# The last product of a fused attention and MLP kernel, moved to seven block products over stored operands

## The chip, the cores and the metric

The kernel runs on one core of one Trainium2 chip, in float32 with matmuls in the float32r form. The metric is the device time of one execution in microseconds, the median of several. Three runs of the kernel before gave 779.0, 778.12 and 778.18, a median of 778.18 us.

## The reference

Attention over 32 memory slots per head, then two MLPs. The first multiplies two projections with each other, the second has a leaky ReLU. Only the last two lines below belong to the stage that is changed; `h` and `o` are the names that the kernel uses for their two products.

```python
def _moe2_ref(x, w_in, w_out):          # x: 2304 x 512, w_in: 512 x 2048, w_out: 2048 x 512
    h = x @ w_in
    g = np.maximum(0.01 * h, h)
    return (g @ w_out).astype(np.float32)
```

The weights come as float64 and are made into float32 on the chip.

## The kernel before

Every float32 operand of a large product is split into a high part (rounded to float32r by ScalarE) and a low part (the rest, by VectorE). A product of two such operands is three matmuls: high by high, high by low, low by high (`PASSES`).

**First part of the program (to about 397 us).** Attention and the first MLP (`ab`, `x1p`) are written as steps with costs, due times and dependencies; `Plan.order` sorts them, and they are issued in that order. Steps of the same plan prepare the weights of the second MLP: `Conv` loads a float64 tile of 512 KB into one of five places called `stage`, two ScalarE operations and one VectorE operation (`join`, L273) make a float32 tile of it, and further operations split it. `plan_pair` does this for two column blocks of `w2_in`, forms the four sums S1 to S4 that Strassen's algorithm (Winograd's form) needs, splits all operands and stores them to a scratch tensor in DRAM (`a_scr`). `plan_w2o` does it for one row block of `w2_out`; 14 of the 16 blocks go through DRAM (`o_scr`), and all 16 are in SBUF from the first quads of the last stage on (`load_w2o`, L1057).

**Last stage (397 us to the end).** Tokens are taken in three rounds `r` of two blocks of 384; the 2048 inner columns in eight pairs `mp` of 128-column blocks. One (round, pair) is a quad, so there are 24. For a quad, `h` is made by seven block products in two PSUM banks (L1231, `mul`, 6 matmuls of 384 columns each), with VectorE sums between them; `leaky` (L1237) writes each of the four blocks of g as a high part and as float32, and a later VectorE subtraction (L1243) gives the low part. `emit_o` (L1247) then multiplies one block of g with its row block of `w2_out`: 9 matmuls of 512 columns (3 token groups by 3 passes, L1254), accumulated over all 16 blocks in six PSUM tiles, `o`. Four such products per quad are placed between the products of `h` of the next one. `store_out` copies a finished `o` to SBUF and writes it out.

The operands of `h` come back from DRAM for every quad: `load_ring` (L1034) refills one part of a two-deep ring as soon as the quad that used it has gone past, on SyncE's queue.

In the last stage the source order is a wish; the framework's scheduler sets the order on each engine.

Of the kernel before, what the change touches and what calls it, by code (L numbers as in the profile page):

```python
# [176 lines left out]
def kernel(  # L177
# [41 lines left out]
    TB = 384  # L219
# [3 lines left out]
    WARM = 27.0  # L223
    scale = 1.0 / float(D) ** 0.5
# [693 lines left out]
    a_scr, o_scr, a_kept, o_kept = {}, {}, {}, {}  # L918

    def plan_pair(mp, due):  # L920

        c, js = {}, []
        holds = [Hold("stage", 5), Hold("stage", 4)]
        convs = []
        for i in range(2):
            m = 2 * mp + i
            view = w2_in[:, m * 128:(m + 1) * 128].rearrange("(t p) c -> p t c", p=128)
            conv = Conv(("w2i", m), view, None, 2)
            convs.append(conv)
            load = plan.add(  # L930
                DMA, 1.46, lambda conv=conv, h=holds[i]: conv.load(f"stage{h.place}"), [s_p2], take=holds[i], due=due
            )
            v = plan.add(ACT, t_act(512), conv.high_word, [load])
            z = plan.add(ACT, t_act(512), conv.low_word, [load])
            js.append(plan.add(DVE, t_dve(512), conv.join, [v, z]))

        def a(i, k):
            return convs[i].hw.bitcast(F32).rearrange("p (a k c) -> p a k c", a=2, k=2)[:, :, k]
# [7 lines left out]
        for n, (ops, after) in enumerate((  # L946
            ((("S1", (1, 0), (1, 1), ALU.add), ("S2", "S1", (0, 0), ALU.subtract)), js),
            ((("S3", (0, 0), (1, 0), ALU.subtract), ("S4", (0, 1), "S2", ALU.subtract)), js),
        )):
            before, users = plan.slot(f"ob{n}")  # L950
            for i, (name, x, y, op) in enumerate(ops):
# [9 lines left out]
                give = [holds[z[0]] for z in {z for z in (x, y) if not isinstance(z, str)}]  # L961
                uses = [users] + [made[z].users for z in (x, y) if isinstance(z, str) and made[z].users is not users]
                made[name] = plan.add(DVE, t_dve(256), add, after + before + need, give=give, uses=uses)
                made[name].users = users
        for i, part in enumerate(PARTS):
            tag = f"X{i}"
            before, users = plan.slot(tag)
            lows = []
            for o, name in enumerate(part):

                def high(i=i, o=o, name=name, tag=tag, part=part):
                    if o == 0:
                        c["out", i] = p2[0].tile([128, len(part), 2, 2, 128], F32R, tag=tag, name="a_out")
                    act.activation(out=c["out", i][:, o, :, 0], in_=src(name), func=ACTF.Copy)

                def low(i=i, o=o, name=name):
                    t = c["out", i][:, o]
                    dve.tensor_tensor(out=t[:, :, 1], in0=src(name), in1=t[:, :, 0].bitcast(F32), op=ALU.subtract)

                direct = name[0] == "A"  # L980
# [7 lines left out]
            def store(i=i, part=part):  # L988
                t = a_scr[mp, i] = scr.tile([128, len(part), 2, 2, 128], F32, tag=f"a{mp}_{i}", name="a_scr")
                dma.dma_start(out=t, in_=c["out", i].bitcast(F32))  # L990

            a_kept[mp, i] = plan.add(DMA, 0.73 * len(part), store, lows, uses=[users], due=due)

    def plan_w2o(m, due):

        before, users = plan.slot(f"R{m % 2}")

        def make():
            t = w2o_t[m] = p2[0].tile([128, 2, DM], F32R, tag=f"R{m % 2}", name="w2o")
            return t[:, 0], t[:, 1]  # L1000

        plan_conv(Conv(("w2o", m), w2_out[m * 128:(m + 1) * 128, :], make, 2), before + [s_p2], users, due=due)
        if m >= 2:

            def store():
                t = o_scr[m] = scr.tile([128, 2, DM], F32, tag=f"o{m}", name="o_scr")
                dma.dma_start(out=t, in_=w2o_t[m].bitcast(F32))

            o_kept[m] = plan.add(DMA, 1.46, store, conv_end["w2o", m], uses=[users], due=due)

    w2o_order = [*range(2, NM), 0, 1]
    for mp in range(NP):
        due = clock[0] - 20.0 + 2.0 * mp
        plan_pair(mp, due)
        for m in w2o_order[2 * mp:2 * mp + 2]:
            plan_w2o(m, due + 6.0)
# [39 lines left out]

    def load_w2o(m):  # L1057
        if m < 4:
            if m == 2:
                w2o_t["AT"] = keep.tile([128, 2, 2, DM], F32R, tag=f"AT{B - 1}", name="w2o")  # L1060
            t = w2o_t["AT"][:, m - 2]
        else:
            tag = f"B{m - 4}" if m < 4 + FH else f"G{m - 4 - FH}"
            t = keep.tile([128, 2, DM], F32R, tag=tag, name="w2o")
        dma.dma_start(out=t.bitcast(F32), in_=o_scr[m])
        w2o_t[m] = t

    s = []
    for m in (2, 3):
        s = [plan.add(  # L1070
            DMA, 1.46, lambda m=m: load_w2o(m), ab_end[B - 1] + [o_kept[m]] + s, due=clock[0] + 8.0 * m - 10.0
        )]

# [126 lines left out]
    p2 = p2[0]  # L1200
    ps2 = ctx.enter_context(tc.tile_pool(name="ps2", bufs=1, space=bass.MemoryType.PSUM, reuse_waits="tile"))
    for m in range(4, NM):
        load_w2o(m)
    banks = [ps2.tile([128, TB], F32, tag=f"h{i}", name="h") for i in range(2)]
    w_tiles = [keep.tile([128, 2 * TB], F32, tag="W", name="sums", bufs=2) for _ in range(2)]
# [3 lines left out]
    gg_tags = [f"stage{i}" for i in range(NS) if i != s4.place]  # L1209

    sums = {"s": w_tiles[0][:, :TB], "U2": w_tiles[0][:, TB:]}
    sums["U3"] = keep.tile([128, TB], F32, tag="t0", name="U3", bufs=2)
    sums["C11"] = keep.tile([128, TB], F32, tag="t0", name="C11", bufs=2)
    u2 = [sums["U2"], keep.tile([128, TB], F32, tag="t1", name="U2")]
    O, GG = {}, {}
    o_todo, o_made = deque(), defaultdict(int)
    later = deque()

    def flush():
        while later:  # L1220
            later.popleft()()

    def mul(bank, n, i, fresh):
# [3 lines left out]
        for kp in range(2):  # L1227
            x = x_halves(op_b)
            x = x[0][:, kp] if len(x) == 1 else x[kp][:, 0]
            for hw, hx in PASSES:  # L1230
                pe.matmul(  # L1231
                    out=banks[bank], lhsT=ring[i % 2, part][:, o, kp, hw], rhs=x[:, hx],
# [4 lines left out]
    def leaky(src, g32, t, m, slot):  # L1237

        gg = GG[t, m] = keep.tile([128, 2, TB], F32R, tag=gg_tags[slot], name="gg")
        act.activation(out=gg[:, 0], in_=src, func=ACTF.Prelu, alpha=0.01)  # L1240
        act.activation(out=g32, in_=src, func=ACTF.Prelu, alpha=0.01)  # L1241
        later.append(
            lambda: dve.tensor_tensor(out=gg[:, 1], in0=g32, in1=gg[:, 0].bitcast(F32), op=ALU.subtract)  # L1243
        )
        o_todo.append((t, m))

    def emit_o(t, m, us=range(TB // 128)):  # L1247
        for u in us:
            n = o_made[t, u]
            o_made[t, u] += 1  # L1250
            if n == 0:
                O[t, u] = ps2.tile([128, DM], F32, tag=f"o{t % 2}{u}", name="o")
            for hg, hw in PASSES:
                pe.matmul(  # L1254
                    out=O[t, u], lhsT=GG[t, m][:, hg, 128 * u:128 * u + 128], rhs=w2o_t[m][:, hw],
                    start=(n == 0 and (hg, hw) == PASSES[0]), stop=(n == NM - 1 and (hg, hw) == PASSES[-1]),
                )
            if n == NM - 1:
                store_out(t * TB + u * 128, O[t, u], u)
# [3 lines left out]
    def store_out(t0, ps, u):  # L1263
        if t0 < NT - 2 * TB:
# [116 lines left out]
```

## Time and profile before

| | |
|---|---|
| median of 3 runs | 778.18 us (778.12 to 779.0) |
| profiled execution, first to last instruction | 776.8 us |
| TensorE busy | 768.3 us, 99% |
| VectorE busy | 422.1 us, 54% |
| ScalarE busy | 379.1 us, 49% |
| DRAM read, written | 103.55 MB, 26.74 MB |

The page gives the span of one profiled execution and no other time for it; the median of the timed runs is 1.4 us above that span. TensorE is busy in nearly all of the span, so the question for any change is how long its instructions take and whether it is made to wait. In the names of the trace, SPq is SyncE's DMA queue.

### The profile page before, as it was taken

How to read it: one execution, taken by the hardware profiler on the slowest of the kernel's cores; microseconds unless marked ns; L12 is line 12 of the kernel's file. 1: busy time of each engine (PE TensorE's matmuls, PEld its weight loads, DVE VectorE, ACT ScalarE, POOL GpSimd, SP SyncE). 2: the span in 40 equal slices, each digit the busy share in tenths (PEclk: the TensorE clock that was granted, in tenths of full speed). 3: DMA queues.
4: the chain of work that ended last, by engine and by line, in shares of the span. 5: the costliest groups of instructions: out<-in, count | busy, mean ns of one | idle time of the engine just before them, and what ended most of it. 6: DMA issues, size and time to landing. Idle time of an engine off the chain costs nothing.

```text
span 776.8 us, 14332 instructions
## 1 busy us (share of the span) xinstructions
PE 768.3 (99%) x5814; PEld 691.4 (89%) x5814; DVE 422.1 (54%) x813; ACT 379.1 (49%) x782; POOL 1.2 (0%) x9
## 2 busy tenths in 40 slices
PE   9999999999999999999999999999999999999997
PEld 5599899898998989898999998999999999899996
DVE  5795755646828898998742233383332364233322
ACT  4897444444948687877413223353332254223223
POOL 0000000000000000000000000000000000000000
PEclk9999999999999999999999999999999999999999
DMA  9987205103604998889357333346333336433303
GB/s 317 339 289 231 91 3 184 31 2 100 226 24 151 324 359 306 303 289 379 145 225 290 122 122 122 109 132 195 122 108 123 122 119 179 136 119 119 115 0 82
DMA packets 59265, 131.21 MB, mean 169 GB/s; under 512 B 4672, under 2 KB 27200, under 8 KB 59200
## 3 DMA queue, kind: packets, MB, share of 16 engines
q1 hardware_dynamic: 59120, 130.17, 49.7%
q8 instruction: 46, 0.75, 0.4%
q14 instruction: 19, 0.16, 0.1%
q10 hardware_dynamic: 80, 0.13, 0.0%
HBM read 103.55 MB, written 26.74 MB: 168 GB/s over the span
## 4 chain that ended last, share of the span: by engine, by line
PE 98%; ACT 1%; DVE 0%; issue 0%
PE o L1254 26%; PE h L1231 23%; PE x1p L848 20%; PE ab L791 20%; PE wp L740 3%; PE warm L1188 2%; PE km L479 1%; PE sc L623 1%; PE qT L595 1%; PE aT L690 0%; DVE AT L705 0%; PE kvT L538 0%; PE bc L432 0%; PE sc L629 0%; PE qL L573 0%
## 5 line engine op out<-in xcount | busy, mean ns | idle before, releaser
L1254 PE MATMUL o<-w2o,gg 128*128 128x512 f32 x864 | 213.6, 392 | 0.0
L1254 PEld LDWEIGHTS o<-w2o,gg 128*128 128x128 f32 x864 | 160.9, 188 | 28.8 <-DVE gg L1243 0.4
L791 PEld LDWEIGHTS ab<-AT,W 128*128 128x128 f32 x1152 | 154.0, 188 | 15.5 <-issue 4.2
L848 PE MATMUL x1p<-G,wo 128*128 128x288 f32 x1152 | 164.0, 298 | 0.0
L791 PE MATMUL ab<-AT,W 128*128 128x288 f32 x1152 | 159.7, 297 | 1.0 <-DVE W L759 0.7
L848 PEld LDWEIGHTS x1p<-G,wo 128*128 128x128 f32 x1152 | 154.7, 188 | 5.8 <-issue 3.0
L1231 PE MATMUL h<-T,ring 128*128 128x384 f32 x720 | 141.4, 337 | 0.0
L1231 PEld LDWEIGHTS h<-T,ring 128*128 128x128 f32 x720 | 127.6, 188 | 4.2 <-ACT C L1241 0.3
L1240 ACT ACTIVATE gg<-U 128x384 fp32r<-128x384 f32 x36 | 18.9, 524 | 99.6 <-DVE U L1324 80.9
L1231 PE MATMUL h<-B,ring 128*128 128x384 f32 x288 | 57.7, 336 | 0.0
L1231 PEld LDWEIGHTS h<-B,ring 128*128 128x128 f32 x288 | 51.3, 188 | 3.8
L813 DVE TENSOR_TENSOR g<-a_sb,ab 128x288 f32<-128x288 f32 x96 | 42.6, 449 | 19.2 <-PE ab L791 15.0
L1243 DVE TENSOR_TENSOR gg<-C,gg 128x384 fp32r<-128x384 f32 x24 | 13.4, 559 | 72.0 <-ACT C L1241 72.0
L1240 ACT ACTIVATE gg<-h 128x384 fp32r<-128x384 f32 x24 | 11.8, 492 | 79.4 <-PE h L1231 79.4
L261 ACT ACTIVATE stage<-stage 128x512 f32<-128x512 f32 x68 | 46.5, 684 | 7.1 <-DMA stage<-in_moe_w_out_dram 2.9
L265 ACT ACTIVATE stage<-stage 128x512 int32<-128x512 uint32 x68 | 46.3, 681 | 0.0
L808 ACT COPY a_sb<-ab 128x288 f32<-128x288 f32 x96 | 37.9, 395 | 9.1 <-PE ab L791 8.5
L759 DVE TENSOR_TENSOR W<-wp,W 128x512 fp32r<-128x512 f32 x48 | 32.4, 685 | 17.3 <-ACT W L753 16.8
L827 ACT ACTIVATE G<-g 128x576 fp32r<-128x576 f32 x48 | 33.0, 687 | 16.3 <-DVE g L813 15.9
L831 DVE TENSOR_TENSOR G<-g,G 128x576 fp32r<-128x576 f32 x48 | 36.1, 753 | 8.0 <-ACT G L827 7.7
L753 ACT ACTIVATE W<-wp 128x512 fp32r<-128x512 f32 x48 | 27.9, 598 | 20.7 <-PE wp L740 11.6
L1324 DVE TENSOR_TENSOR U<-U,h 128x384 f32<-128x384 f32 x24 | 13.3, 554 | 44.9 <-PE h L1231 44.9
(101 smaller groups left out, 656.3 us busy)
## 6 DMA issues: line engine op xcount, KB each, us to landing
ring<-a_scr SPq DMA_DIRECT2D x72, 512.0 KB, 3.5
stage<-in_moe_w_out_dram SPq DMA_DIRECT2D x28, 512.0 KB, 5.4
a_scr<-a_out SPq DMA_DIRECT2D x24, 512.0 KB, 4.6
stage<-in_moe_w_in_dram SPq DMA_DIRECT2D x16, 512.0 KB, 5.7
o_scr<-w2o SPq DMA_DIRECT2D x14, 512.0 KB, 7.9
w2o<-o_scr SPq DMA_DIRECT2D x14, 512.0 KB, 7.1
stage<-in_moe_w_a_dram SPq DMA_DIRECT2D x12, 512.0 KB, 5.8
stage<-in_moe_w_b_dram SPq DMA_DIRECT2D x12, 512.0 KB, 5.6
```

The costliest lines, as they stand in the source:

```text
L261: act.activation(out=x, in_=x, func=ACTF.Prelu, scale=2.0 ** -112, alpha=2.0 ** 32)
L265: act.activation(out=self.lw, in_=self.lw.bitcast(U32), func=ACTF.Copy, scale=7.249 / 2.0 ** 32, bias=0.25)
L759: dve.tensor_tensor(out=t[:, 1], in0=c["ps"][:, :, 256 * i:256 * i + 256], in1=t[:, 0].bitcast(F32), op=ALU.subtract)
L791: pe.matmul(out=c[x, n][:, :HS], lhsT=W[b, f][:, hw, g, 128 * x:128 * x + 128], rhs=AT[b][:, g, ha, n * HS:(n + 1) * HS], start=(g == 0 an ...
L808: act.copy(c["sb"][:, n], c[0, n][:, :HS])
L813: dve.tensor_tensor(out=c["g"][:, n], in0=c["sb"][:, n], in1=c[1, n][:, :HS], op=ALU.mult)
L827: act.activation(out=G[b, f][:, 0], in_=c["g"], func=ACTF.Copy)
L831: dve.tensor_tensor(out=t[:, 1], in0=c["g"], in1=t[:, 0].bitcast(F32), op=ALU.subtract)
L848: pe.matmul(out=c[n][:, :HS], lhsT=wo_t[f][:, hw, 128 * m:128 * m + 128], rhs=G[b, f][:, hg, n], start=(f == fs[0] and (hw, hg) == PASSES[0]),
L1231: pe.matmul(out=banks[bank], lhsT=ring[i % 2, part][:, o, kp, hw], rhs=x[:, hx], start=fresh and kp == 0 and (hw, hx) == PASSES[0], stop=k ...
L1240: act.activation(out=gg[:, 0], in_=src, func=ACTF.Prelu, alpha=0.01)
L1254: pe.matmul(out=O[t, u], lhsT=GG[t, m][:, hg, 128 * u:128 * u + 128], rhs=w2o_t[m][:, hw], start=(n == 0 and (hg, hw) == PASSES[0]), stop= ...
```

## The change

`o` is made by one level of Strassen's algorithm too (Winograd's form: seven products in place of eight).

- The blocks of g of a quad are a 2 by 2 matrix: two token blocks by two column blocks. `w2_out` of the same pair is a 2 by 2 matrix of 128 by 256 blocks. Each product is 9 matmuls of 256 columns (3 token groups by 3 passes).
- Quads are taken in chunks of four. For a chunk, product 1 is done for its four quads one after another into the same PSUM accumulator, then product 2, and so on (`o_product`, 28 steps). After each group of four, VectorE or ScalarE adds or copies 768 columns of PSUM to running totals C11, C12, C21, C22 in SBUF (`o_sums`). Two chunks make a round; then totals are stored.
- The products of `o` of a chunk are placed beside the products of `h` of the next chunk: 28 steps of one `h` product (6 matmuls) and one `o` product (9 matmuls). The first chunk has `h` alone, with its quads taken two at a time in four PSUM banks; after the last chunk `o` is alone.
- `leaky` now writes float32 alone. VectorE makes S1 to S4 of g (`g_sum`, one operation of 384 columns each), and every operand is split for itself (`g_split`: ScalarE high, VectorE low, 384 columns each).
- The operands of `w2_out` (four blocks and four sums, T1 to T4, all split) are made by `plan_pair`, stored in DRAM, and read back for each product: 168 loads of 256 KB (`load_t`), into four places at first and eight later. Four of the eight pairs are prepared in the first part of the program as before; the other four (`LATE = 4`) are prepared during the first chunks of the last stage, their steps spread between the products (0.9 of a planned microsecond per step, `tempo`).

The core of the diff:

```diff
-    def emit_o(t, m, us=range(TB // 128)):
-        for u in us:
...
-            for hg, hw in PASSES:
-                pe.matmul(
-                    out=O[t, u], lhsT=GG[t, m][:, hg, 128 * u:128 * u + 128], rhs=w2o_t[m][:, hw],
...
+    def g_split(c, k):
+        n, q = divmod(k, 4)
+        name = O_OPS[n][0]
+        src, t = g[4 * c + q, name], s_slots.popleft()
+        s_op[c, k] = t
+        act.activation(out=t[:, 0], in_=src, func=ACTF.Copy)
+        dve.tensor_tensor(out=t[:, 1], in0=src, in1=t[:, 0].bitcast(F32), op=ALU.subtract)
...
+    def load_t(c, k):
...
+        dma.dma_start(out=t.bitcast(F32), in_=o_scr[4 * (c % 2) + q, part][:, o])
...
+        for u in range(3):
+            for hs, ht in PASSES:
+                pe.matmul(
+                    out=acc[chain][:, 256 * u:256 * u + 256], lhsT=s[:, hs, 128 * u:128 * u + 128], rhs=t[:, ht],
...
+    tempo = 0.0
+    for c in range(chunks + 1):
+        for k in range(steps):
+            if c == 0:
+                pair, n = divmod(k, 14)
+                n, which = divmod(n, 2)
+                h_product(2 * pair + which, n, pairs[which], w_sets[which])
+            elif c < chunks:
+                q, n = divmod(k, 7)
+                i = 4 * c + q
+                h_product(i, n, banks, {**w_sets[0], "U2": w_sets[i % 2]["U2"]})
+                if later:
+                    later.popleft()()
+                if c % 2 and c + 1 < chunks:
+                    x_ready_next(c // 2, q, n)
+            if c:
+                o_product(c - 1, k)
+                o_ready(c - 1, k)
...
+            if now >= -AHEAD:
+                advance(now, AHEAD, g_split, s_slots)
+                advance(now, T_AHEAD, load_t, t_slots)
+            if late:
+                tempo += 0.9
+                while late and late[0].start < tempo:
+                    late.popleft().emit()
```

**TensorE, in the middle of the last stage.** Before, two products of `h` (L1231) and one of `o` (L1254) in turn:

```order
L1231 MATMUL h<-B_4874,ring 128x384 x6
L1231 MATMUL h<-T_4936,ring 128x384 x6
L1254 MATMUL o<-w2o,gg 128x512 x9
L1231 MATMUL h<-B_5000,ring 128x384 x6
L1231 MATMUL h<-T_5014,ring 128x384 x6
L1254 MATMUL o<-w2o,gg 128x512 x9
```

Now, one product of `h` (L1241) and one of `o` (L1330) in turn:

```order
L1241 MATMUL h<-B_5204,ring 128x384 x6
L1330 MATMUL o<-w2o,S 128x256 x9
L1241 MATMUL h<-T_5226,ring 128x384 x6
L1330 MATMUL o<-w2o,S 128x256 x9
L1241 MATMUL h<-B_5242,ring 128x384 x6
L1330 MATMUL o<-w2o,S 128x256 x9
```

A quad had four products of `o` and has seven; each is half as wide.

**VectorE, from the last addition of the first MLP (L869, now L871) into the first quads of the last stage.** Before, sums of `h` (L1305, L1315, L1324, L1328), low parts of g (L1243) and two sums for later rounds (L1097):

```order
L869 TENSOR_TENSOR x_2983<-x_2983,x1p 128x288 x8
L1097 TENSOR_TENSOR sums<-x_2239,x_1563 128x768
L1097 TENSOR_TENSOR T<-x_2239,sums 128x768
L1305 TENSOR_TENSOR sums<-sums,h 128x384
L1243 TENSOR_TENSOR gg<-C_5420,gg 128x384
L1315 TENSOR_TENSOR U_5419<-sums,h 128x384
L1324 TENSOR_TENSOR U_5419<-U_5419,h 128x384
```

Now the sums of `h` (L1260, L1264) stand behind work for the late pairs (sums L975, low parts L1000, join L275):

```order
L871 TENSOR_TENSOR x_2983<-x_2983,x1p 128x288
L1000 TENSOR_TENSOR w2o<-S,w2o 128x256
L1000 TENSOR_TENSOR w2o<-stage,w2o 128x256 x2
L975 TENSOR_TENSOR S<-stage 128x256
L1088 TENSOR_TENSOR sums<-x_2239,x_1563 128x768
L975 TENSOR_TENSOR S<-stage,S 128x256
L275 SCALAR_TENSOR_TENSOR stage<-stage 128x512
L975 TENSOR_TENSOR S<-stage,S 128x256
L1260 TENSOR_TENSOR sums<-sums,h 128x384
L1000 TENSOR_TENSOR w2o<-stage,w2o 128x256
L1000 TENSOR_TENSOR w2o<-S,w2o 128x256
L1260 TENSOR_TENSOR U_5419<-g,h 128x384
```

Seven instructions for the late pairs and one for a later round have come between the last addition to x and the first sum of `h` there, where two for a later round stood.

**SyncE's queue in the second chunk.** Before, ring loads alone (L1039):

```order
L1039 DMA ring<-a_scr 128x1024 x3
L1039 DMA ring<-a_scr 128x512
L1039 DMA ring<-a_scr 128x1024 x3
L1039 DMA ring<-a_scr 128x512
L1039 DMA ring<-a_scr 128x1024 x3
```

Now ring loads (L1048), stores of the late pairs (L1014) and loads of operands for `o` (L1303), in one queue:

```order
L1303 DMA w2o<-a_scr 128x512 x2
L1014 DMA a_scr<-w2o 128x512
L1048 DMA ring<-a_scr 128x1024
L1303 DMA w2o<-a_scr 128x512 x2
L1014 DMA a_scr<-w2o 128x1024
L1048 DMA ring<-a_scr 128x1024
L1303 DMA w2o<-a_scr 128x512
L1048 DMA ring<-a_scr 128x512
L1303 DMA w2o<-a_scr 128x512
L1014 DMA a_scr<-w2o 128x1024
```

A load of an operand of `o` now stands behind a store that waits for VectorE, and a ring load behind both.

## Rows read from the trace of the kernel before

**Rows 1.** Page: span, and busy time of each engine with its instructions.
```profile
span 776.8 us, 14332 instructions
...
PE 768.3 (99%) x5814; PEld 691.4 (89%) x5814; DVE 422.1 (54%) x813; ACT 379.1 (49%) x782; POOL 1.2 (0%) x9
```

**Rows 2.** Page: the chain that ended last, by engine and by line.
```profile
PE 98%; ACT 1%; DVE 0%; issue 0%
PE o L1254 26%; PE h L1231 23%; PE x1p L848 20%; PE ab L791 20%; PE wp L740 3%; PE warm L1188 2%; PE km L479 1%; PE sc L623 1%; PE qT L595 1%; PE aT L690 0%; DVE AT L705 0%; PE kvT L538 0%; PE bc L432 0%; PE sc L629 0%; PE qL L573 0%
```

**Rows 3.** Stretches: busy us (instructions) by engine, granted clock, DMA share, GB/s.
```profile
310.00:330.00 20.00, 20.00 (x165) 17.99 (x165) 18.92 (x42) 17.15 (x37) 0.00 (x0) 1.00 0.85 310
...
350.00:370.00 20.00, 20.00 (x166) 17.99 (x165) 16.73 (x34) 15.42 (x31) 0.00 (x0) 1.00 1.01 377
...
400.00:410.00 10.00, 10.00 (x52) 8.83 (x51) 4.89 (x10) 3.94 (x8) 0.00 (x0) 1.00 1.03 416
...
440.00:500.00 60.00, 60.00 (x302) 54.24 (x301) 18.98 (x35) 17.07 (x35) 0.00 (x0) 1.00 0.36 118
```

**Rows 4.** Timeline of TensorE: start us, us, then instructions merged, with count.
```profile
384.81 12.90 PE L848 MATMUL x1p<-G,wo 128*128 128x288 f32 x96
397.55 1.20 PE L1231 MATMUL h<-B,ring 128*128 128x384 f32 x6
...
440.47 1.20 PE L1231 MATMUL h<-B,ring 128*128 128x384 f32 x6
441.51 1.20 PE L1231 MATMUL h<-T,ring 128*128 128x384 f32 x6
442.56 2.21 PE L1254 MATMUL o<-w2o,gg 128*128 128x512 f32 x9
444.61 1.20 PE L1231 MATMUL h<-B,ring 128*128 128x384 f32 x6
```

**Rows 5.** 128-column transposes: their line's durations (min/median/max ns), and three in the timeline.
```profile
L595 PE MATMUL qT<-ident,q_t x64: 270/272/332, 12.1 to 177.6; 128*128 128x128 f32 x64
...
29.81 0.49 PE L595 MATMUL qT<-ident,q_t 128*128 128x128 f32 x3
```

**Rows 6.** Groups of the last stage's matmuls: count, busy us, mean ns, idle before.
```profile
L1254 PE MATMUL o<-w2o,gg 128*128 128x512 f32 x864 | 213.6, 392 | 0.0
...
L1231 PE MATMUL h<-T,ring 128*128 128x384 f32 x720 | 141.4, 337 | 0.0
...
L1231 PE MATMUL h<-B,ring 128*128 128x384 f32 x288 | 57.7, 336 | 0.0
```

**Rows 7.** DMA issues: line, count, KB each, median us to landing; last, 400 to 420 us alone.
```profile
ring<-a_scr SPq DMA_DIRECT2D x72, 512.0 KB, 3.5
...
ring<-a_scr SPq DMA_DIRECT2D x24, 256.0 KB, 2.6
...
ring<-a_scr SPq DMA_DIRECT2D x6, 512.0 KB, 9.7
```

**Rows 8.** VectorE groups by shape: busy us, mean ns of one, idle before and releaser.
```profile
L273 DVE SCALAR_TENSOR_TENSOR stage<-stage 128x512 int32<-128x512 int32 x44 | 30.2, 687 | 4.1 <-ACT stage L265 4.0
...
L1243 DVE TENSOR_TENSOR gg<-sums,gg 128x384 fp32r<-128x384 f32 x36 | 20.1, 558 | 23.9 <-ACT sums L1241 23.9
...
L1324 DVE TENSOR_TENSOR U<-U,h 128x384 f32<-128x384 f32 x24 | 13.3, 554 | 44.9 <-PE h L1231 44.9
...
L978 DVE TENSOR_TENSOR a_out<-S,a_out 128x256 fp32r<-128x256 f32 x32 | 12.8, 417 | 0.2 <-ACT a_out L974 0.2
...
L1123 DVE TENSOR_TENSOR T<-T,T 128x768 fp32r<-128x768 f32 x10 | 9.5, 950 | 0.0
```

**Rows 9.** Timeline where the first MLP ends: VectorE's last addition to x.
```profile
397.75 0.45 DVE L869 TENSOR_TENSOR x<-x,x1p 128x288 f32<-128x288 f32 x1 [1.95 <-PE x1p L848]
```

**Rows 10.** Timeline of the end: the last matmuls and the last copy.
```profile
763.85 8.61 PE L1254 MATMUL o<-w2o,gg 128*128 128x512 f32 x36
...
772.49 0.59 ACT L1269 COPY ob<-o 128x512 f32<-128x512 f32 x1 [2.13 <-PE o L1254]
```

**Rows 11.** Waits of SyncE's queue: us in total, times, longest us.
```profile
SPq L1039 <- PE h L1231: 269.6, 82, 3.8
```

More of the change, by code (lines that the diff above doesn't have):

```diff
@@ L945, in plan_pair @@
         made = {}
[L946 to L949, printed above, removed]
+        for n, ops in enumerate(sums):
             before, users = plan.slot(f"ob{n}")
@@ new lines, in o_sums @@
+    def o_sums(c, n):
+        src = acc[O_OPS[n][2]][:, :768].rearrange("p (u c) -> p u c", u=3)
+        first = c % 2 == 0
+        for name, fresh in (
+            (("C11", first),), (("C22", first),), (("C21", first),), (("C21", False),),
+            (("C22", False), ("C12", first)), () if first else (("C11", False),), (("C12", False),),
+        )[n]:
+            if fresh:
+                act.copy(total[name], src)
+            else:
+                dve.tensor_tensor(out=total[name], in0=total[name], in1=src, op=ALU.add)
+        done = {3: "C21", 4: "C22", 5: "C11", 6: "C12"}.get(n)
+        if done and not first:
+            store_out(c // 2, done)
@@ new lines, with store_out @@
+    out_v = out.rearrange("(b p j) c -> b j p c", b=B, p=64)
+    def store_out(r, name, us=range(3)):
+        row, col = int(name[1]) - 1, int(name[2]) - 1
+        for u in us:
+            for h in range(2):
+                b, j = divmod((2 * r + row) * (TB // 64) + 2 * u + h, NR)
+                queue = act if h and len(us) == 1 else dma
+                queue.dma_start(
+                    out=out_v[b, j][:, 256 * col:256 * col + 256], in_=total[name][64 * h:64 * h + 64, u]
+                )
@@ new lines, with add, late_steps @@
+    class Late(Plan):
+        def add(self, engine, cost, emit, after=(), uses=(), **kw):
+            return super().add(engine, cost, emit, [x for x in after if x is not s_p2], uses, **kw)
+    late_plan = Late(stage=0)
+    late_plan.places["stage"] = [(0.0, i) for i in places]
+    for mp in range(NP - LATE, NP):
+        late_holds = plan_pair(late_plan, "out", mp, 100.0 * mp, ("R0", "R1", f"B{FH - 2}", f"G{FH - 1}"))
+    late = deque(late_plan.order())
+    def late_steps(until):
+        while late and late[0].start < until:
+            late.popleft().emit()
@@ L1341, with advance, x_ready_next @@
+    following = {g_split: 0, load_t: 0}
+    def advance(now, ahead, make, slots):
+        while following[make] <= min(now + ahead, chunks * steps - 1) and len(slots) > 1:
+            make(*divmod(following[make], steps))
+            following[make] += 1
+    def x_ready_next(r, q, n):
+        if q == 2 and n == 6:
             for name in ("T1", "T2", "T3"):
                 t_make(r + 1, name)
-        if not last:
-            o_next()
-    flush()
-    for n in range(2):
-        rest = [x for x in o_todo if x[0] == NTB - 2 + n]
-        for u in range(TB // 128):
-            for x in rest:
-                emit_o(*x, [u])
+        if q == 3:
+            if n == 3:
+                while later:
+                    later.popleft()()
+                t_make(r + 1, "T4")
+            x_split(r + 1, X_NAMES[n], False)
+            later.append(lambda: x_split(r + 1, X_NAMES[n], True))
```

335 lines of the change are left out of this document (184 added, 151 removed).

## The prediction, made before the changed kernel ran

> **What bounds the kernel now.** First the page's busy shares: TensorE works in 99% of the span [rows 1]; then the chain of waits: 98% of it is TensorE, and the two products of the last stage are its longest entries, `o` with 26% and `h` with 23% [rows 2]. Then the stretches: at 400 to 410 and at 440 to 500 us TensorE is busy for the whole stretch at a granted clock of 1.00, the 2.4 GHz level, while VectorE has about a third of its time taken [rows 3]. The groups of the three matmul forms have no idle time before them [rows 6]. So the last stage is as long as its matmuls are, and a change there is worth what it takes out of TensorE's column time, less every wait that it brings.
>
> **Matmuls.** A matmul's own duration (392 ns for 512 columns, [rows 6]) overlaps the next one, so I take distances between starts in the timeline [rows 4]: 288 columns (397.55 - 384.81) / 96 = 132.7 ns; 384 columns (441.51 - 440.47) / 6 = 173.3 ns; 512 columns (444.61 - 442.56) / 9 = 227.8 ns. The three lie on a line of 0.42 ns per column. No matmul of 256 columns of this kind is in the trace. The line gives 132.7 - 32 x 0.423 = 119.2 ns. Its bounds are the nearest rows on both sides: not above the 132.7 of 288 columns, not below the 109 ns at which 128-column transposes follow each other ((490 - 272) / 2, [rows 5]).
>
> `o` had 864 matmuls [rows 6]: 864 x 227.8 = 196.8 us. It gets 24 quads x 7 products x 9 = 1512: 1512 x 119.2 = 180.2 us. **Gain 16.6 us**; between the bounds, from a gain of 32.0 (109 ns) to a loss of 3.8 (132.7 ns). `h` keeps its 1008 matmuls of 384 columns.
>
> **First part of the program.** VectorE loses 16 joins and 16 low parts of 512 columns, 32 x 0.687 = 22.0 us, and gets four pairs of 2 joins and 11 operations of 256 columns: 4 x (2 x 0.687 + 11 x 0.417) = 23.8 us [rows 8]. That is the same load in the same place: 0.
>
> **First chunks: two new loads at once.** The first chunk has only `h`, so a step is 6 x 173.3 = 1.04 us instead of a quad's mixture, and the four late pairs are prepared there.
>
> VectorE: between its last addition to x and the last sum of the first quad stand 15 operations of 256 columns, 2 joins, 2 of 768, 9 sums of `h` and 2 splits: 15 x 0.417 + 2 x 0.687 + 2 x 0.950 + 9 x 0.554 + 2 x 0.558 = 15.6 us [rows 8]. It starts on them 0.65 us after the first matmul of `h` (398.20 against 397.55, [rows 9, 4]), so it ends at 16.3. TensorE wants that bank for its 15th product, at 14 x 1.04 = 14.6: **1.7 us late**. The next two quads have 11 us of VectorE work for 14.6 of TensorE.
>
> DMA: from the fifth load for a late pair to the point where the operands of `o` get eight places in place of four, SyncE's queue has 4 late loads (2.1 MB), 16 late stores (7.3), 25 ring loads (11.5) and 20 operand loads (5.2): 26.2 MB. TensorE needs 48 products of `h` and 16 of `o` for that: 48 x 1.04 + 16 x 9 x 0.1192 = 67.1 us. With all engines of the DMA taken the trace shows 377 GB/s in loads mixed with stores and 416 in loads alone [rows 3]: 69.5 or 63 us, so 2.4 us too late or nothing. The lowest rate near there is 310, with a DMA share of 0.85 [rows 3]: 84.5 us, 17.4 late. I take 377, the row with the same mixture: **2.4 us**. While the queue is full a ring load lands after 9.7 us instead of 3.5 [rows 7], and with four places an operand of `o` is asked for only three products ahead, some 7 us; so the wait would be seen before products of `o`. A store that waits for VectorE holds back every load behind it in the same queue; SyncE already spends 269.6 us waiting for `h` before ring loads [rows 11]. The Trainium skill, page "DMA: Bandwidth & Descriptors", section "Where 436 GB/s comes from", says that between HBM and SBUF some 358 GB/s per core are the limit; by that figure the 26.2 MB take 73.2 us (an estimate from the page) and the wait is 6.1. The trace's 377 and 416 exceed it, so this sum does not use it.
>
> The two waits partly cover each other: together **4**, from 0 to 17.4.
>
> **Middle of the stage.** Per quad VectorE gets 7 splits, 4 sums of g and 5 sums of `h`, and totals of 768 columns: about 10 to 11 us against 7 x 1.04 + 7 x 1.073 = 14.8 on TensorE. Operand loads add 7 x 0.262 MB per 14.8 us, 124 GB/s to the 118 of now [rows 3]: 242 of 377. Both hidden: 0. ScalarE has no more than VectorE: 0.
>
> Where a round ends, the operands of the next are prepared too. In quads 8 and 9 of the 24 VectorE has 49 operations of 384 columns or their equal and 10 of 768: 49 x 0.556 + 10 x 0.950 = 36.7 us, against 14 products of `h` and 18 of `o`, 33.9: 2.8 short. In quads 16 and 17 it is 30.5 against 29.6: 0.9 short. VectorE takes its work in order, and between the last product of one quad and the first of the next there is one product of `o`, 1.07 us, for the sum that frees the bank. Together 3.7, taken as **4**; from 0 (the quads before have room) to 19.6, when all the preparation (11.1 and 8.5 us) is exposed.
>
> **End.** The last chunk has `o` alone: VectorE 25 us for TensorE's 31, and operands asked for six steps, 6.4 us, ahead of loads that land in 2.6 in this size [rows 7]. After the last matmuls came a copy and a store [rows 10], now an addition and a store. **1**.
>
> **Sum.** 776.8 - 16.6 + 4 + 4 + 1 = 769.2 for the profiled span. The median of the runs is 1.4 above the span shown, so **770.6 us**.
>
> **Rivals.**
> - *All hidden.* Both DMA and VectorE keep up, and only the matmuls change: 776.8 - 16.6 + 1 + 1.4 = 762.6. For it: the scheduler lays `o` products late in the second chunk, which gives early transfers time. Against: VectorE's counts above leave no room at two places. 20%.
> - *DMA sets the pace of the first two chunks (slower).* At 310 GB/s the wait there is 17.4: 776.8 - 16.6 + 17.4 + 4 + 1 + 1.4 = 784. It decides for slower when that wait exceeds 16.6 - 5 = 11.6 us, which is 26.2 MB at under 333 GB/s. For it: three kinds of transfers in one queue, in order, with stores that wait. Against: 377 and 416 in the trace. 17%.
> - *VectorE's order.* Half of the preparation for the next round is exposed, 9.8 in place of 4, and the first chunk stays at 4: about 776.4; with all of it 786. 10%.
> - *Weight loads do not get shorter with the columns.* Each matmul has a load of 128 columns of weights before it, and there are 648 more of them; if the pair cannot go below 132.7, `o` takes 200.6 us and the time is 776.8 + 3.8 + 9 + 1.4 = 791. Against: the 109 ns of 128-column transposes, with such a load before each. 5%. The Trainium skill, page "TensorE: Matmul & The Clock Gate", section "LDWEIGHTS (loading the stationary operand)", gives columns / 1.2 in ns, an estimate of 107 ns for 128 columns: the transposes' 109 agree with it as a floor, and 256 columns would be just above it.
>
> **Chances and range.** The forecast 48%, the rivals as given. A difference of 0.2%, 1.6 us, is about what a measurement of this kernel can tell. Faster by more than that: nearly all of the forecast (46), all hidden (20) and a little of VectorE's order (1): 67%. Within 0.2%: 7%, the edge of the forecast and part of VectorE's order. Slower: 26%, DMA, weight loads, the rest of VectorE's order and of the forecast. The range of 762 to 784 takes in the first three rivals up to their values, but neither the weight loads nor full exposure of the preparation.
>
> **What would show it.** Right: starts of 256-column matmuls about 119 ns apart; TensorE without idle time from the third chunk on except at two round ends; a DMA share of 1 for some 60 us from 397 us on, with short waits of `o` for operand loads or of `h` for VectorE. Wrong: starts at 130 ns or more; waits for DMA of over 10 us; waits spread over all quads, which would mean that banks, not preparation, hold TensorE; or a granted clock below 1.00 after a wait.

## The result, and the profile after

The changed kernel takes **772.09 us** (median of 4 runs, 770.9 to 773.19) against 778.59 for the kernel before in the same session: a ratio of 0.9913, 95% interval 0.9894 to 0.9932. It is 6.5 us faster; 7.6 were forecast. The profiled execution spans 771.4 us, 5.4 less than before; it is the slowest of the four (773.19 us), so what is read from it below accounts for 5.4 us and not for the 6.5 of the medians. The sum behind the forecast is not the sum that came out.

The page of the changed kernel: span, busy time of each engine, the chain by engine and by line, two groups of matmuls (count | busy us, mean ns of one | idle before), and the DMA issues (count, KB, median us to landing).

```profile
span 771.4 us, 16541 instructions
...
PE 753.5 (98%) x6462; PEld 709.5 (92%) x6462; DVE 549.4 (71%) x1082; ACT 424.0 (55%) x894; POOL 1.2 (0%) x9
...
PE 88%; DMA 6%; ACT 2%; DVE 2%; SPq 1%; issue 1%; ACTq 0%; DVEq 0%
PE o L1330 22%; PE ab L793 20%; PE h L1241 19%; PE x1p L850 18%; PE wp L742 3%; DMA stage<-in_moe_w_out_dram 2%; DMA w2o<-a_scr 2%; DMA stage<-in_moe_w_a_dram 1%; PE sc L625 1%; PE km L481 1%; DMA a_scr<-w2o 1%; PE qT L597 1%; PE warm L1179 1%; PE o L1311 1%; SPq L1364 1%
...
L1330 PE MATMUL o<-w2o,S 128*128 128x256 f32 x1476 | 196.8, 282 | 1.7 <-DMA w2o<-a_scr 1.7
...
L1241 PE MATMUL h<-T,ring 128*128 128x384 f32 x720 | 144.3, 337 | 2.8 <-ACT g L1251 1.6
...
w2o<-a_scr SPq DMA_DIRECT2D x168, 256.0 KB, 4.0
ring<-a_scr SPq DMA_DIRECT2D x72, 512.0 KB, 5.1
```

Where the chain was 98% TensorE [rows 2], DMA has come in with 6%, and the groups of matmuls, which had no idle time [rows 6], have some. The stretches say where it is (columns as in [rows 3]):

```profile
397.00:427.00 30.00, 27.33 (x151) 25.54 (x150) 24.18 (x53) 16.07 (x36) 0.00 (x0) 1.00 0.91 304
427.00:460.00 33.00, 30.27 (x198) 28.97 (x198) 21.63 (x48) 16.91 (x37) 0.00 (x0) 1.00 0.97 347
460.00:475.00 15.00, 14.18 (x98) 13.46 (x97) 9.47 (x20) 7.64 (x18) 0.00 (x0) 1.00 0.90 296
475.00:500.00 25.00, 24.99 (x184) 24.79 (x183) 24.01 (x44) 17.41 (x33) 0.00 (x0) 1.00 0.94 341
...
600.00:622.00 22.00, 22.00 (x159) 22.00 (x158) 21.24 (x43) 14.22 (x29) 0.00 (x0) 1.00 0.75 247
...
735.00:772.00 37.00, 29.27 (x228) 28.55 (x226) 20.14 (x35) 9.99 (x19) 0.00 (x0) 0.93 0.63 182
```

TensorE is idle for 6.2 us between 397 and 475 us, never at the two round ends, and again in the last 15 us. Between, it is full.

**Matmuls.** In the timeline of the changed kernel's TensorE, steps of `h` and `o` follow each other thus:

```profile
491.74 1.23 PE L1330 MATMUL o<-w2o,S 128*128 128x256 f32 x9
492.81 1.21 PE L1241 MATMUL h<-T,ring 128*128 128x384 f32 x6
493.86 1.22 PE L1330 MATMUL o<-w2o,S 128*128 128x256 f32 x9
```

(492.81 - 491.74) / 9 = 118.9 ns for 256 columns; over the 100 undisturbed groups of nine from 500 to 735 us the mean is 1.067 us, 118.6 ns. `h` stays at 1.05.

**The first two chunks.** ScalarE and SyncE's queue in the changed kernel's timeline, at the two longest stops of TensorE there (in brackets the idle time before the instruction and what ended it):

```profile
399.32 0.68 ACT L263 ACTIVATE stage<-stage 128x512 f32<-128x512 f32 x1 [1.28 <-DMA stage<-in_moe_w_out_dram]
399.90 0.67 ACT L267 ACTIVATE stage<-stage 128x512 int32<-128x512 uint32 x1
400.46 0.46 ACT L1258 COPY sums<-h 128x384 f32<-128x384 f32 x1
...
401.47 0.46 ACT L1258 COPY g<-h 128x384 f32<-128x384 f32 x1
...
421.03 0.43 ACT L997 ACTIVATE w2o<-stage 128x256 fp32r<-128x256 f32 x1 [4.24 <-DMA a_scr<-w2o]
421.37 0.48 ACT L1251 ACTIVATE g<-h 128x384 f32<-128x384 f32 x1
...
422.30 0.47 ACT L1251 ACTIVATE g<-h 128x384 f32<-128x384 f32 x1
```

```profile
410.92 3.57 SPq L1048 DMA_DIRECT2D ring<-a_scr  x4
414.58 0.38 SPq L1014 DMA_DIRECT2D a_scr<-w2o  x1
```

```profile
401.98 1.32 PE L1241 MATMUL h<-T,ring 128*128 128x384 f32 x6 [1.22 <-ACT g L1258]
...
422.83 7.47 PE L1241 MATMUL h<-T,ring 128*128 128x384 f32 x40 [1.41 <-ACT g L1251]
```

ScalarE takes its work in order. At 421 it splits a late operand into a place that an earlier late operand still holds, until its store has landed; that store was issued at 414.58, behind four ring loads, and took over 6 us. Behind the split stand the operations (L1251) that free `h`'s banks; TensorE goes on after the second, at 422.83. At 399 ScalarE waits for a late load, and the copies (L1258) stand behind it and behind other late work.

These are two of several stops. All waits of TensorE from 397 to 475 us (us in total, times, longest):

```profile
PE o L1330 <- DMA w2o<-a_scr: 1.7, 2, 1.2
PE h L1241 <- ACT sums L1258: 1.6, 2, 1.0
PE h L1241 <- ACT g L1251: 1.6, 2, 1.4
PE h L1241 <- ACT g L1258: 1.2, 1, 1.2
```

The stop at 422 is the only one that ends directly behind a late store (1.41 us; 0.15 in a second profile of the same kernel). The others end on loads of operands of `o`, or on operations of ScalarE that stand behind its other work, the late pairs' own splits and conversions among it.

**The end.** The changed kernel's TensorE and then SyncE's queue, from the last products on:

```profile
743.74 14.12 PE L1330 MATMUL o<-w2o,S 128*128 128x256 f32 x117
757.70 0.52 PE L1311 MATMUL o<-w2o,S 128*128 128x256 f32 x3
759.07 1.30 PE L1311 MATMUL o<-w2o,S 128*128 128x256 f32 x9 [0.85 <-DMA w2o<-a_scr]
762.88 4.75 PE L1311 MATMUL o<-w2o,S 128*128 128x256 f32 x24 [2.50 <-DMA w2o<-a_scr]
```

```profile
750.28 3.68 SPq L1364 DMA_DIRECT2D out_dram<-C  x6
754.06 1.03 SPq L1303 DMA_DIRECT2D w2o<-a_scr  x2
755.17 4.39 SPq L1364 DMA_DIRECT2D out_dram<-C  x6
759.66 1.02 SPq L1303 DMA_DIRECT2D w2o<-a_scr  x2
760.77 7.81 SPq L1364 DMA_DIRECT2D out_dram<-C  x9
```

The last 36 matmuls take 9.9 us from first start to last end; without waits, in a run below, they take 4.6. The last four operand loads stand in SyncE's queue behind twelve stores of 64 KB, one every 0.6 to 0.7 us. And the last 24 matmuls take 4.75 us, 198 ns each. The stretches of 1 us show why (the value after POOL is the granted clock):

```profile
762.00:763.00 1.00, 0.12 (x1) 0.15 (x2) 0.00 (x0) 0.00 (x0) 0.00 (x0) 1.00 0.85 299
763.00:764.00 1.00, 1.00 (x6) 1.00 (x7) 0.00 (x0) 0.00 (x0) 0.00 (x0) 0.61 0.64 181
764.00:765.00 1.00, 1.00 (x6) 1.00 (x6) 0.12 (x1) 0.00 (x0) 0.00 (x0) 0.50 0.43 97
```

After the wait of 2.5 us the clock is at 0.50, the 1.2 GHz level, until 766.6; that costs 4.75 - 24 x 0.119 = 1.9 us.

### The profile page after: what moved, and what is told of

The parts are those of the page before. It is cut to its first block, busy times and chain, and to the rows that moved or that the text cites. A ratio compares the mean times of both kernels' runs of the same rounds, so it can differ in the third digit from the quotient of the medians.

```text
span 771.4 us, 16541 instructions
## 1 busy us (share of the span) xinstructions
PE 753.5 (98%) x6462; PEld 709.5 (92%) x6462; DVE 549.4 (71%) x1082; ACT 424.0 (55%) x894; POOL 1.2 (0%) x9
## 4 chain that ended last, share of the span: by engine, by line
PE 88%; DMA 6%; ACT 2%; DVE 2%; SPq 1%; issue 1%; ACTq 0%; DVEq 0%
PE o L1330 22%; PE ab L793 20%; PE h L1241 19%; PE x1p L850 18%; PE wp L742 3%; DMA stage<-in_moe_w_out_dram 2%; DMA w2o<-a_scr 2%; DMA stage<-in_moe_w_a_dram 1%; PE sc L625 1%; PE km L481 1%; DMA a_scr<-w2o 1%; PE qT L597 1%; PE warm L1179 1%; PE o L1311 1%; SPq L1364 1%
## 5 line engine op out<-in xcount | busy, mean ns | idle before, releaser
L1330 PE MATMUL o<-w2o,S 128*128 128x256 f32 x1476 | 196.8, 282 | 1.7 <-DMA w2o<-a_scr 1.7
L1330 PEld LDWEIGHTS o<-w2o,S 128*128 128x128 f32 x1476 | 191.7, 190 | 2.3 <-DMA w2o<-a_scr 2.3
L1241 PE MATMUL h<-T,ring 128*128 128x384 f32 x720 | 144.3, 337 | 2.8 <-ACT g L1251 1.6
L1294 DVE TENSOR_TENSOR S<-g,S 128x384 fp32r<-128x384 f32 x168 | 92.6, 556 | 73.5 <-ACT S L1293 73.1
L1293 ACT ACTIVATE S<-g 128x384 fp32r<-128x384 f32 x168 | 87.2, 521 | 102.1 <-PE o L1330 99.6
L1241 PEld LDWEIGHTS h<-T,ring 128*128 128x128 f32 x720 | 121.5, 189 | 5.0 <-ACT g L1251 2.5
L1241 PE MATMUL h<-B,ring 128*128 128x384 f32 x288 | 58.7, 338 | 1.7 <-ACT sums L1258 1.6
L1284 DVE TENSOR_TENSOR g<-g 128x384 f32<-128x384 f32 x96 | 52.4, 554 | 3.4 <-ACT g L1251 2.4
L1241 PEld LDWEIGHTS h<-B,ring 128*128 128x128 f32 x288 | 48.3, 188 | 3.0 <-ACT sums L1258 2.3
L1351 DVE TENSOR_TENSOR C<-C,o 128x768 f32<-128x768 f32 x32 | 30.2, 953 | 12.6 <-PE o L1330 11.7
```

The source lines that it names most:

```text
L1241: pe.matmul(out=out, lhsT=ring[i % 2, part][:, o, kp, hw], rhs=x[:, hx], start=fresh and kp == 0 and (hw, hx) == PASSES[0], stop=kp == 1 a ...
L1284: dve.tensor_tensor(out=t, in0=x, in1=y, op=op)
L1293: act.activation(out=t[:, 0], in_=src, func=ACTF.Copy)
L1294: dve.tensor_tensor(out=t[:, 1], in0=src, in1=t[:, 0].bitcast(F32), op=ALU.subtract)
L1330: pe.matmul(out=acc[chain][:, 256 * u:256 * u + 256], lhsT=s[:, hs, 128 * u:128 * u + 128], rhs=t[:, ht], start=fresh and q == 0 and u != ...
```

## The experiments

Each is the changed kernel with an edit, run beside the kernel before. The cost of a disturbed stretch is read in two ways: as TensorE's idle time, and, more exactly, from starts in the timeline: time between two starts less the number of matmuls between them times 173.3 (384 columns) or 119 ns (256). The second also holds gaps that show as busy, because a matmul's own duration (282 ns for 256 columns) reaches 0.16 us beyond the start of the next. By starts the changed kernel loses 9.5 us from 397 to 475 us where it shows 6.2 idle, and a second profile of it (`after_again`) loses 7.7 where it shows 4.4.

**The yardstick.** The changed kernel once more.

> The changed kernel unaltered, as the yardstick for the others on one chip: 771 to 773 us, with 6 us of TensorE's idle time in 397 to 475 us and waits of 3.4 us before the last matmuls.

Measured: 771.65 us (6 runs, 770.35 to 774.26), ratio 0.9905 [0.9887, 0.9923]; idle time of 4.4 us and waits of 2.9 us before the last matmuls, the clock at 0.50 again.

**No late work.** `late.popleft()` in place of `late.popleft().emit()`, and

```diff
-        dma.dma_start(out=t.bitcast(F32), in_=o_scr[4 * (c % 2) + q, part][:, o])
+        dma.dma_start(out=t.bitcast(F32), in_=o_scr[q, part][:, o])
```

> The preparation of the four late pairs (loads, ScalarE and VectorE work, stores) is left out, and the operands of the four early pairs are read in their place: the preparation of four of the eight pairs of w2_out is left out. Theory (the 6.2 us that TensorE is idle between 397 and 475 us come from the late pairs' work alone): TensorE is idle there for under 1 us, and the time is about 6 us under the changed kernel, 766 us. Rival (the idle time comes from the seven products of h in four banks, or from operand loads as such): 4 us or more of the idle time stay, 770 us or more.

Measured: 762.5 us, ratio 0.9788 [0.9775, 0.9801]. TensorE has no idle time left from 397 to 735 us. The first product of `h` and the first of the last 36 matmuls in this kernel's timeline:

```profile
396.64 2.24 PE L1241 MATMUL h<-B,ring 128*128 128x384 f32 x12
...
747.49 0.52 PE L1311 MATMUL o<-w2o,S 128*128 128x256 f32 x3
```

They are 350.85 us apart; in the changed kernel 757.70 - 397.16 = 360.54. The same matmuls lie between, so **the late work costs 9.7 us** (7.9 by the second profile), and the whole of the time lost there comes from it. The rival falls. The expected 6 us was TensorE's idle time; the starts show half as much again.

**No late stores.** The late pairs are loaded and split, but not stored; the same edit of `load_t`, and

```diff
-                    late.popleft().emit()
+                    x = late.popleft()
+                    if x.engine != DMA or x.take:
+                        x.emit()
```

> The late pairs are loaded, summed and split on ScalarE and VectorE as in the changed kernel, but not stored, and the operands of the early pairs are read in their place: the stores of four pairs are left out. Theory (stores in SyncE's queue are what makes loads late and holds ScalarE, whose late conversions stand before the work that frees a bank): 3 to 6 us under the changed kernel, 766 to 769 us. Rival (ScalarE's and VectorE's own work for the late pairs holds TensorE): under 2 us less, 770 to 772 us, with the same waits of h for ScalarE.

Measured: 765.03 us, ratio 0.9824 [0.9806, 0.9841]; lost by starts, 1.8 us. VectorE and ScalarE are busier here in the first chunk than in the changed kernel, and TensorE is not held:

```profile
397.00:427.00 30.00, 29.14 (x168) 28.09 (x168) 29.64 (x72) 22.92 (x54) 0.00 (x0) 1.00 0.83 291
427.00:460.00 33.00, 33.00 (x232) 33.00 (x232) 23.66 (x46) 16.62 (x33) 0.00 (x0) 1.00 0.88 293
```

So it is mainly the stores, not the arithmetic: VectorE works 29.64 of 30 us there, and that stretch loses 1.7 us by starts. More than half of what is left is one stop of 0.86 us at 402.8, for the same copy (L1258): ScalarE stands at no load before it here, and the copy comes behind late splits and conversions. So the wait for the load at 399 in the changed kernel is not the only way to this stop.

**Thin late stores.** Every store keeps its place and its waits, with a small part of its bytes; the same edit of `load_t`.

```diff
+                src = c["out", i].bitcast(F32)
+                if not inner and mp >= NP - LATE:
+                    t, src = t[:, :1, :1, :128], src[:, :1, :1, :128]
+                dma.dma_start(out=t, in_=src)
```

> Every late store stays in its place in SyncE's queue with its waits, but writes 128 columns of one part of one operand, 64 KB in place of 256 or 512 KB, and the operands of the early pairs are read in their place: seven eighths or three quarters of the late stores are left out. Theory A (bytes: the DMA engines are full from 397 to 475 us, so loads and stores take longer and ScalarE waits for them): as without the stores, TensorE is idle for about 1 us in 397 to 475 us, 765 to 766 us. Theory B (order: a store that waits for VectorE holds back the loads behind it in the queue): as with the full stores, 5 to 6 us idle, 771 to 772 us.

Measured: 767.78 us, ratio 0.9852 [0.9835, 0.9868]; lost by starts, 4.3 us, between the 1.8 without stores and the 7.7 to 9.5 with full ones. Neither theory alone: more than half of what the stores cost goes with their bytes, the rest (4.3 - 1.8) stays with their place in the queue, their issue or their landing; the bytes from 397 to 475 us are nearly those of the run without stores, 22.6 against 22.2 MB.

**Late stores from GpSimd's queue.**

```diff
-                dma.dma_start(out=t, in_=c["out", i].bitcast(F32))
+                queue = dma if inner or mp < NP - LATE else nc.gpsimd
+                queue.dma_start(out=t, in_=c["out", i].bitcast(F32))
```

> The late pairs' stores are issued from GpSimd's queue instead of SyncE's; all bytes stay. Theory (the place in SyncE's queue delays them): 2 to 4 us under the changed kernel, 768 to 770 us, and ScalarE's wait of 4.2 us for a late store is gone. Rival (the 16 DMA engines are full in that stretch, DMA share 0.9 to 0.97, so the order of issue is worth nothing): 772 us within 1 us.

Both missed: 778.39 us, ratio 0.9999 [0.9986, 1.0011]: the whole gain is gone. The timeline of this kernel at its longest stop:

```profile
418.41 0.42 ACT L997 ACTIVATE w2o<-S 128x256 fp32r<-128x256 f32 x1 [1.96 <-DMA a_scr<-w2o]
...
418.86 0.43 DVE L1000 TENSOR_TENSOR w2o<-S,w2o 128x256 fp32r<-128x256 f32 x1 [1.84 <-ACT w2o L997]
...
421.20 0.55 DVE L1273 TENSOR_TENSOR U<-U,h 128x384 f32<-128x384 f32 x1
...
421.80 2.29 PE L1242 MATMUL h<-B,ring 128*128 128x384 f32 x6 [2.98 <-DVE U L1273]
```

The chain is the same, one engine longer: a store that has not landed stops ScalarE, ScalarE stops VectorE, and the sum that frees the bank comes late. From 397 to 460 us a late store of 512 KB needs 7.2 us to land, in the changed kernel 5.6. After the stop the clock is at 0.50:

```profile
423.00:424.00 1.00, 1.00 (x5) 1.00 (x4) 0.95 (x3) 0.00 (x0) 0.53 (x1) 0.50 0.60 227
```

The schedule of VectorE and ScalarE differs too in this kernel, and the low clock has its part, so how much of the 16 us lost by starts is the queue's alone stays open.

**Stores of the last round held back.**

```diff
-            store_out(c // 2, done)
+            if c == chunks - 1:
+                held.append(done)
+            else:
+                store_out(c // 2, done)
...
+                while held and following[load_t] == chunks * steps:
+                    store_out(chunks // 2 - 1, held.popleft())
```

> Last round's stores of C21, C22 and C11 are issued only when every operand load of o has been issued. Theory (the last four loads come late because they stand in SyncE's queue behind 12 small stores, and the clock falls in the wait): the waits of the last 36 matmuls for loads, 0.85 and 2.50 us, and the time at a granted clock under 0.9, some 2 us, go; the stores at the very end may give back up to 2 us. 3 to 5 us under the changed kernel, about 767 to 769 us. Rival (the loads are late because the transfers themselves are slow there, whatever the order): no change, 772 us, same two waits.

Measured: 769.92 us, ratio 0.9890 [0.9877, 0.9903], 2 us under the changed kernel; the intervals overlap, so the trace has to decide. TensorE and SyncE's queue at the end of this kernel (span 767.9):

```profile
756.84 4.63 PE L1312 MATMUL o<-w2o,S 128*128 128x256 f32 x36
```
```profile
753.12 12.19 SPq L1368 DMA_DIRECT2D out_dram<-C  x19
```

The 36 matmuls take 4.63 us in place of 9.9: the waits and the low clock came from the order in the queue. But 19 stores take 12.2 us to issue, 0.64 each, and the end is 6.4 us behind the last matmul, where the changed kernel has 3.8.

**Stores merged as well.** Two to four DMAs for a total in place of six.

```diff
+        if len(us) == 3:
+            for h in range(2):
+                at = [divmod((2 * r + row) * (TB // 64) + 2 * u + h, NR) for u in us]
...
+                    dma.dma_start(
+                        out=out_v[b, j:j + 2 * n - 1:2].rearrange("u p c -> p u c")[:, :, 256 * col:256 * col + 256],
+                        in_=total[name][64 * h:64 * h + 64, u:u + n],
+                    )
```

> Stores of output totals are merged: two to four DMAs in place of six for each total, and in the last round they are held until the operand loads have been issued. Theory (SyncE needs 0.6 us for each small store, so 19 of them at the end take 12 us): the stores after the last matmul end sooner; 2 to 4 us under the kernel that only holds them back (769.9), about 767 us. Rival (the last landing sets the end, not the issue): 769 to 770 us, with 4 to 6 us between the last matmul and the end as now.

Measured: **765.68 us**, ratio 0.9826 [0.9811, 0.9840]; faster than both kernels, 6.4 us under the changed one. The last matmul ends at 760.4, the span at 764.1. From the first of the last 36 matmuls to the end of the span it is 8.3 us, against 13.7 and 13.0 in the two profiles of the changed kernel: some 5 us of the 6.4 are the end's. The first chunks still lose 7.6 us by starts.

```profile
755.76 4.63 PE L1312 MATMUL o<-w2o,S 128*128 128x256 f32 x36
```

**Two late pairs in place of four** (`LATE = 2`, with the merged stores).

> With merged and held stores, and two late pairs in place of four: two more pairs are prepared in the first part of the program. Theory (the late pairs' transfers, 2.1 MB of loads and 3.7 MB of stores less after 397 us, are what fills the DMA): TensorE's idle time in 397 to 475 us falls from 6.2 to under 2 us, and the first part hides 12 us more of VectorE's work (busy 88% from 250 to 350 us): 4 to 5 us under the kernel with merged stores. Rival (VectorE has no room in the first part): the first product of h of the last stage starts up to 12 us later than at 397.2, and the time rises by up to 8 us.

Measured: 767.81 us, ratio 0.9851 [0.9832, 0.9871]: 2 us slower than with four, with intervals that overlap a little. With two more pairs to prepare, the first part takes 3.1 us longer, as this kernel's timeline of TensorE shows; before its first product of `h` it waits for the split of x, which stands on ScalarE:

```profile
400.21 0.62 PE L1241 MATMUL h<-B,ring 128*128 128x384 f32 x2 [0.57 <-ACT B L1116]
```

and 397 to 475 us still lose 7.5 us, with almost as many bytes there (25.8 MB against 25.3): half the late stores are gone, but those left land later (512 KB after 8.2 us, 5.7 with four late pairs).

**Other paces of the late work** (with the merged stores): `tempo` 0.75 and 1.05; begun 2 planned us later; 1.2.

> With merged and held stores, and the late work spread more evenly: 0.75 planned us a step in the first chunk (one product a step) and 1.05 in the second (two products), in place of 0.9 in both. Theory (the DMA engines are full for the sum of the bytes from 397 to 475 us): within 1 us of the kernel with merged stores, 765.7. Rival (the first chunk alone is crowded, with half the time for a step): TensorE's idle time in 397 to 427 us, 1.4 us with merged stores, falls under 0.5 us, that in 397 to 475 us from 4.6 to under 3 us; 1.5 us or more under 765.7.

> With merged and held stores, and the late work begun 2 planned us later, at the same 0.9 a step. Theory (at the first product ScalarE, in order, stands at a late pair's load that has not landed while a copy that frees h's bank is behind it): the idle time of 1.1 us near 402 us goes, about 1 us under 765.7. Rival (the wait moves with the work and turns up some products later): 765.7 within 0.7 us.

> With merged and held stores, and the late work hurried: 1.2 planned us a step in both chunks. Theory (more late bytes and more of ScalarE's and VectorE's work per step than the first chunk holds): TensorE's idle time in 397 to 475 us rises from 4.6 to 8 us or more, 769 us or more, perhaps with a granted clock under 1.00. Rival (the eight places for operands of o and the four more for splits, which come when the late work is done, are worth more than the crowding costs): under 765.7.

Measured: 770.06, 767.18 and 766.58 us, ratios 0.9885 [0.9861, 0.9909], 0.9842 [0.9826, 0.9858] and 0.9841 [0.9823, 0.9860]; by starts 13.4, 9.0 and 9.0 us lost from 397 to 475. None beats 765.68; the last two are not told apart from it. Begun later, the wait at the first product is still there (1.1 us at 402.5); hurried, the waits move from loads to VectorE's sums. The even pace makes it worse, against the rival. Its profile is of the slowest of six executions (774.96 us), so the 13.4 is too much for the median; in it four waits of `o` for loads follow (3.0 us), and one of 2.0 us for ScalarE, after which the clock is at 0.50. That the late work ends later, and operands of `o` have four places until then, would explain the waits for loads, but no run sets it apart. The pace moves the loss, it does not remove it.

**More work for VectorE at the round ends** (with the merged stores).

```diff
-            later.append(lambda: x_split(r + 1, X_NAMES[n], True))
+            later.append(lambda: [x_split(r + 1, X_NAMES[n], True) for _ in range(2)])
```

> With merged and held stores; the low parts of x's operands for the next round are computed twice, the same values: 6.9 and 7.1 us more for VectorE where the two rounds end. Theory (VectorE is full there, 28.3 of 30 us from 480 to 510 and 19.3 of 20 from 600 to 620, and its order, by which sums of h come between the preparation, only spreads the work): VectorE stays full some 7 us longer and TensorE waits for sums of h or for splits for 2 us or more at one round end at least, 768 us or more. Rival (TensorE is far from waiting there, because the operands are wanted later than they are made): TensorE idle under 0.5 us at either, 765.7 within 1 us.

Measured: 767.69 us, ratio 0.9863 [0.9847, 0.9880], 2.0 us more, but not there:

```profile
480.00:510.00 30.00, 29.91 (x218) 29.70 (x217) 30.00 (x53) 17.52 (x34) 0.00 (x0) 1.00 0.86 307
...
600.00:620.00 20.00, 20.00 (x144) 19.79 (x144) 19.95 (x39) 12.34 (x25) 0.00 (x0) 1.00 0.76 247
```

VectorE is busy without a gap, and TensorE is idle for 0.09 us. The theory falls: TensorE is far from waiting there. The two profiled executions are 1.2 us apart: 0.8 is a later start of the last stage (397.9 against 397.1), and by starts 0.2 us more are lost up to 475 us and 0.25 behind. The rest of the 2.0 is not placed.

## Why the prediction was right, and where it was not

The time fell inside the range, 1.5 us beside the forecast. The mechanism holds in outline (shorter matmuls, less what the late work costs), but each term was off, and that they cancelled is luck.

- **Matmuls, 16.6 forecast, about 19.4 measured.** 256 columns: 119.2 forecast, 118.6 measured. Rows on both sides and a line through three widths were enough, and weight loads set no floor above it. The size that was off is the old one: I took one row of 512 columns, 2.05 us for nine [rows 4]; over 54 groups of nine in 500 to 735 us the mean is 2.066, 229.6 ns. That gives 198.4 - 179.3 = 19.1. From starts alone: the kernel without late work needs 350.85 us up to the last 36 matmuls, the one before 763.85 - 397.55 = 366.30 [rows 4, 10], and the last 36 of each add 36 x 0.111 = 4.0: 19.4.
- **First chunks, 4 forecast, 9.7 measured.** The step that failed is the one on VectorE's 15 operations and the bank (1.7 us late): TensorE does not stop at its 15th product, and none of its waits there ends on VectorE. They end on ScalarE (4.4 us) and on loads of `o` (1.7). The text named late stores only as "A store that waits for VectorE holds back every load behind it"; without them 1.8 of the 9.5 us are left. By which way they cost the most (one place held until a store has landed, loads behind stores, or bytes) the runs split only in part: with thin stores 4.3 us are left. The DMA term counted right and failed in its form. From the fifth late load, issued at 395.8, to 473.3 us the trace has the transfers that I counted but for one operand load, at 316 GB/s and a DMA share of 0.92. That is below my threshold of 333, and yet the direct waits of `o` for loads were 1.7 us, not over 11.6, and the queue itself stands waiting for 37 us until TensorE has done with a place and for 11 us for VectorE. What the waits show is the way from issue to landing, 5.6 us for a late store, with an engine standing behind it; the landing itself was not slower than that of 512 KB stores in the kernel before (medians of 4.6 and 7.9 us for its two kinds). Since a share of 0.92 leaves little room, how much of the landing time is a matter of the rate stays open.
- **The figure of 358 GB/s** from the Trainium skill, page "DMA: Bandwidth & Descriptors", section "Where 436 GB/s comes from", gave a wait of 6.1 us as an estimate. The traces go beyond it in stretches of 10 and 20 us (416 and 377 before [rows 3]), so it is no limit for these. The mean of 316 here lies under it, and whether it holds over a longer stretch no run shows.
- **Round ends, 4 forecast, 0.3 measured.** VectorE was as full as I counted (24.0 of 25 us, 21.2 of 22). The step that failed is that "there is one product of `o`, 1.07 us, for the sum that frees the bank": with 14 us more of preparation (6.9 and 7.1) TensorE was idle there for under 0.1 us. The reason, that the preparation may lag by several products because its operands are wanted only in the next round, is argued and not shown.
- **End, 1 forecast, 4.7 measured.** 5.3 us in the last 36 matmuls (waits, 3.4; clock, 1.9), less 0.6 after them. I priced the loads by their landing (2.6 us, asked 6.4 us ahead) and the issue of DMAs at nothing; twelve small stores ahead of the loads in the same queue were not counted. The prediction named "a granted clock below 1.00 after a wait" as a sign against it, and it came.
- **Sum.** 776.8 - 19.4 + 9.7 (round ends in it) + 4.7 - 0.4 (the last stage starts earlier) = 771.4, the span. In the second profile the first chunks take 1.8 us less, and its span is 768.8.
- **Rivals.** "All hidden" did not occur in the changed kernel. The run without late work meets its 762.6 with 762.5, by chance: the matmuls gave more and the end cost more than it says. With the end mended it is 765.7. "DMA sets the pace" had the place right and the price wrong. "VectorE's order" did not occur. The rival on weight loads is refuted by the 118.6 ns.

## What to carry to other kernels

Count for each queue what is issued ahead of the transfer that is wanted, and price the issue (here 0.3 to 0.7 us each), not only bytes and landing: merging small stores and issuing the last ones behind the last loads was worth 6.4 us by the medians, some 5 of them at the end, nearly as much as the whole change. When work is spread into a full stage, ask for each in-order engine what it stands behind: a buffer that comes free only when a store has landed can stop ScalarE, then VectorE, then TensorE (seen at 421 us here, and with stores from GpSimd's queue), while an engine that is merely full (VectorE at the round ends) may cost nothing. Profile a kernel twice before a stop of 1 us is explained: one of the stops here was gone in the second profile. Read a loss from the starts of matmuls, since idle time alone showed two thirds of it or less.

## What had not been expected of the hardware

- SyncE's issue of a DMA took 0.32 us (median) for operand loads of 256 KB and 0.59 (0.47 to 1.31) for output stores of 64 KB with rows of 1 KB; the issuing queue can be what is short while the 16 engines are not (DMA share 0.63 in the last 37 us).
- After TensorE had stood for 2.50 us (changed kernel), 1.66 us (its second profile), 1.71 us (no late stores) and 2.98 us (stores from GpSimd's queue), the granted clock was at 0.50, the 1.2 GHz level, for 3 to 6 us more, although TensorE worked through; with GpSimd's queue it fell again at 448 us, after a stop of 1.35 us that came soon after one of 1.43. After stops of 1.2 and 1.4 us near 402 and 422 us, and of 1.72 us in the kernel without late work, it stayed at 1.00. The length of the last stop alone does not tell the two apart here.
- With the late stores issued from GpSimd's queue, transfers from 397 to 460 us landed later: a ring load of 512 KB after 6.5 us (5.7 in the changed kernel), a late store after 7.2 (5.6).
